# Cross attention with a gelu MLP on one core: the x loads moved to step 0, the x^T transposes behind them, two Strassen products swapped, and the read-out rows stored in one transfer

## The chip, the cores and the metric

The kernel runs on one core of a Trainium2 chip. The metric is the time of one execution on the device in microseconds (us). Every duration below is from one profiled execution of the kernel before, whose own time is 220.42 us.

## The reference

For each of 8 batches and 8 heads, x (512 rows of 64) attends to a state of 32 rows, and the state attends back to x. Both read-outs are joined (512 + 32 = 544 rows a batch, 512 columns) and go through a two-layer MLP with an exact gelu.

```
scores  = x @ state^T / 8 ;  a  = softmax(scores)  ; xread = a  @ state     # 512 rows a batch
scores2 = state @ x^T / 8 ;  a2 = softmax(scores2) ; sread = a2 @ x         # 32 rows a batch
X = concat([xread, sread]) as (8*544, 512)
out = gelu(X @ w_in) @ w_out          # w_in 512x2048, w_out 2048x512
```

## The kernel before, in words

The read-out is never formed for the 512 rows: P = state @ w_in is made per batch (`p_mm`, L415), and hidden = A @ P needs only A^T, the transposed softmax weights (`mm1`, L478, two matmuls for each of 16 blocks m; ScalarE applies the gelu, L485, into `g`). The second layer multiplies `g` by w_out. For batches 0 and 1 it is a plain product (`mm2`, L504). From batch 2 on it is one level of a Strassen scheme: seven products 3, 4, 5, 2, 1, 7, 6 of half size (`X`, matmuls L602), whose left sides are sums of parts of `g` (`g_sum`, VectorE, L596) and whose results are combined on their way out. Call them M1 to M7. Each has a fixed PSUM bank: M3 and M5 use bank 0, M4 and M2 bank 1, M1 and M7 bank 2, M6 bank 3. M7 accumulates onto what M1 left, so `q`, which reads M1 from the bank (L646), must have read it before M7 starts.

The order is written out by hand. The loop at L842 runs over slots b = 2 to 7. A slot has 8 steps p; a step runs two blocks of layer one of batch b (`M(k, k+1)`), and then one Strassen product of batch b-1 (steps 0 to 4) or of batch b (M3 at step 6, M6 at step 7). In its gaps a slot also prepares batch b+1 (scores at step 1, softmax norm at steps 2 and 3, A^T at step 5, P at steps 5 and 7) and loads x for batch b+3. Slot 1 is written the same way ahead of the loop (L817 to L840). In the profile, slot 2 starts at 58.7 us, slot 3 at 80.7, slot 4 at 103.2, slot 5 at 126.8 and slot 6 at 149.1.

What runs on the queues around the change:

- GpSimd (POOL): `load_x(b)` issues the x load of a batch (L117, 512 KB, with a cast to bf16), after a one-element copy to `hold` (L839, L880) that makes the queue wait for a gelu result. `rearr` copies x into the layout `x4` (L218, two copies), `rearr_ones` into `xo` (L228, two copies), and the Strassen terms `u` (L641) and `v` (L648) are subtractions.
- SyncE (SP) only issues transfers, in order: the DMA transposes xT <- x4 (L271, for the scores of that batch) and AT <- a (L367), and the stores of results. A transfer waits in the queue until its data is ready, and everything behind it waits too.
- VectorE (DVE) runs, among others, norm (cs, ics, a: L344 to L347), g_sum, q, the read-out pieces inv, srm and XSR (L391, L392, L405), the two final sums of a batch `oh` (L652, L656) and half of the P copies (L427).

Within slot b, step 0 begins with `rearr` and `xtr_dma` of batch b+2; step 2 ends with `rearr_ones` of batch b+2 and then `hold` (on gelu block 4 of the slot) and `load_x(b+3)`. After the loop come the last products and the 256 read-out rows: `mm2_sr(s)` for four batches at a time, which ends in `evac` (a copy out of PSUM and one store for each batch's 32 rows). `X7_split` stores the last half in pieces.

Of the kernel before, what the change touches and what calls it, by code (L numbers as in the profile page):

```python
# [9 lines left out]
FP32 = mybir.dt.float32  # L10
BF16 = mybir.dt.bfloat16
AF = mybir.ActivationFunctionType
ALU = mybir.AluOpType
# [4 lines left out]
def kernel(  # L18
# [8 lines left out]
    nc = tc.nc  # L27
# [87 lines left out]
    def load_x(b):  # L115
        xb = xin.tile([128, H, SJ * D], BF16, name="xb", tag="xb")
        nc.gpsimd.dma_start(out=xb, in_=xr[b])  # L117
        xbs[b] = xb
# [80 lines left out]
    def begin(b):  # L199
        A = Att()  # L200
        atts[b] = A
        A.x4 = x4s[b % 2]
        A.xo = xos[b % 2]
        if b > 0:
            A.xT = att.tile([128, SJ, HC, 128], BF16, name="xT", tag="xT")
# [8 lines left out]
    def rearr(b):  # L214
        A = atts[b]
        src = xbs[b].rearrange("p (t c) (j d) -> p t c j d", t=2, d=D)
        for t in range(2):
            nc.gpsimd.tensor_copy(  # L218
                out=A.x4[:, :, :, 64 * t:64 * t + 64].rearrange("p j c d -> p c j d"),
                in_=src[:, t],  # L220
            )
# [47 lines left out]
    def xtr_dma(b):  # L269
        A = atts[b]  # L270
        nc.sync.dma_start_transpose(  # L271
            out=A.xT.rearrange("p j c n -> p (j c) n"),
            in_=A.x4.rearrange("p j c n -> p (j c n)"),
        )
# [214 lines left out]
    def evac(ps, rows):  # L489
        osb = opool.tile([128, d_model], FP32, name="osb", tag="osb")  # L490
        nc.vector.tensor_copy(out=osb, in_=ps)
        for r, src, n0, n1 in rows:
            nc.sync.dma_start(out=r, in_=osb[src, n0:n1])
# [34 lines left out]
    def mm2_sr(s):  # L528
        ps = ps_f.tile([128, d_model], FP32, name="ops", tag="f")
        for m in range(MC):  # L530
            nc.tensor.matmul(  # L531
                ps,
                lhsT=g_sr[:, m, s * 128:(s + 1) * 128],
                rhs=w_out_bf[:, m, :],
                start=(m == 0),
                stop=(m == MC - 1),
            )
        rows = []
        for i in range(4):
            r0 = (4 * s + i) * SB + S  # L540
            rows.append((out[r0:r0 + NS, :], slice(32 * i, 32 * i + 32), 0, d_model))
        evac(ps, rows)


    def mm2_m(b, m):
# [65 lines left out]
    def c_tile(name):  # L611
        return cpool.tile([128, 2, NH], FP32, name=name, tag=name)

    def x_out(b, h):
        rows = out[b * SB:b * SB + S, :].rearrange("(p j) n -> p j n", j=SJ)
        nc.sync.dma_start(out=rows[:, 2 * h:2 * h + 2, :], in_=xs[b, "o", h])

    def X(b, name):
        bank = {"3": 0, "4": 1, "5": 0, "2": 1, "1": 2, "6": 3, "7": 2}[name]
        first = name in "3416"  # L620
        if first:
            xs[b, bank] = otile([128, 2, NH], "xp", bank)
        ps = xs[b, bank]
        lhs = {"3": (0, 0), "4": (1, 1)}.get(name)
        lhs = xs[b, "g" + name] if lhs is None else g_q(b, *lhs)
        rhs = {"5": w_q[1][1], "2": w_q[0][0]}.get(name)
        rhs = w_sum[name] if rhs is None else rhs
        x_mm(ps, lhs, rhs, first)
        if name == "3":
            xs[b, "s3"] = c_tile("s3")  # L630
            nc.scalar.copy(out=xs[b, "s3"], in_=ps)
            for h in range(2):
                xs[b, "o", h] = hpool.tile([128, 2, d_model], FP32, name="oh", tag=f"oh{h}")
        elif name == "4":
            xs[b, "s34"] = c_tile("s34")
            nc.vector.tensor_tensor(out=xs[b, "s34"], in0=ps, in1=xs[b, "s3"], op=ALU.add)  # L636
        elif name == "5":
            o = xs[b, "o", 0][:, :, NH:]
            nc.scalar.copy(out=o, in_=ps)  # L639
            xs[b, "u"] = c_tile("u")  # L640
            nc.gpsimd.tensor_tensor(out=xs[b, "u"], in0=xs[b, "s34"], in1=o, op=ALU.subtract)  # L641
        elif name == "2":
            nc.scalar.copy(out=xs[b, "o", 1][:, :, :NH], in_=ps)
        elif name == "1":
            xs[b, "q"] = c_tile("q")
            nc.vector.tensor_tensor(out=xs[b, "q"], in0=ps, in1=xs[b, "s34"], op=ALU.add)  # L646
            xs[b, "v"] = c_tile("v")
            nc.gpsimd.tensor_tensor(  # L648
                out=xs[b, "v"], in0=xs[b, "q"], in1=xs[b, "o", 1][:, :, :NH], op=ALU.subtract
            )  # L650
        elif name == "7":
            nc.vector.tensor_tensor(  # L652
                out=xs[b, "o", 1][:, :, NH:], in0=xs[b, 3], in1=xs[b, "v"], op=ALU.add
            )
            x_out(b, 1)
            nc.vector.tensor_tensor(  # L656
                out=xs[b, "o", 0][:, :, :NH], in0=ps, in1=xs[b, "u"], op=ALU.add
            )
            x_out(b, 0)
# [7 lines left out]
                out=xs[b, "q"][:, j, :], in0=ps[:, 0, :], in1=xs[b, "s34"][:, j, :], op=ALU.add  # L667
            )

    def c22(b):  # L670
        xs[b, "v"] = c_tile("v")
        o = xs[b, "o", 1]
        nc.gpsimd.tensor_tensor(
            out=xs[b, "v"], in0=xs[b, "q"], in1=o[:, :, :NH], op=ALU.subtract
        )
        nc.vector.tensor_tensor(out=o[:, :, NH:], in0=xs[b, 3], in1=xs[b, "v"], op=ALU.add)
        x_out(b, 1)

    def X7_split(b):
        rows = out[b * SB:b * SB + S, :].rearrange("(p j) n -> p j n", j=SJ)  # L680
        o = xs[b, "o", 0]
        nc.sync.dma_start(out=rows[:, 0:2, NH:], in_=o[:, :, NH:])
        for j in range(2):
            ps = xs[b, "x", j]
            x_mm(ps, xs[b, "g7"], w_sum["7"], False, (j,))
            nc.vector.tensor_tensor(
                out=o[:, j, :NH], in0=ps[:, 0, :], in1=xs[b, "u"][:, j, :], op=ALU.add
            )
            eng = nc.scalar if j else nc.sync
            eng.dma_start(out=rows[:, j, :NH], in_=o[:, j, :NH])  # L690
# [127 lines left out]
    for p in range(2, 8):  # L818
        if p == 4:
            scores(2, 0)  # L820
            scores(2, 1)
            norm(2, 0)
            norm(2, 1)
        if p == 7:
            atr_dma(2)
        if p == 3:
            begin(3)
            rearr(3)
            xtr_dma(3)
            rearr_ones(3)  # L830
        M(16 + 2 * p, 17 + 2 * p)
        U(u)
        u += 1
        if p in (5, 7):
            pmat(2, 2 + p // 7)
        if p >= 3:
            w_sums(p - 3)
        if p == 4:
            nc.gpsimd.tensor_copy(out=hold, in_=gs[1][:, 8, 0:1])  # L839
            load_x(4)  # L840

    for b in range(2, B):  # L842
        nb = b + 1
        for p in range(8):
            k = 16 * b + 2 * p
            if p == 0 and nb + 1 < B:
                begin(nb + 1)
                rearr(nb + 1)
                xtr_dma(nb + 1)
            if p == 1 and nb < B:  # L850
                scores(nb, 0)
                scores(nb, 1)
            if p in (2, 3) and nb < B:
                norm(nb, p - 2)
            if p == 5 and nb < B:
                atr_dma(nb)
            M(k, k + 1)
            if nb == B and p >= 4:
                for m in range(4 * p - 16, 4 * p - 12):
                    mm1_sr(m)  # L860
            if b == 2:
                for _ in range(2 if p < 4 else 1):
                    if u < 32:
                        U(u)
                        u += 1
            elif p < 5:
                if p == 0:
                    g_sum(b - 1, "5")
                X(b - 1, "45217"[p])
                if p < 3:  # L870
                    g_sum(b - 1, "217"[p])
            if p == 1:
                sread(b)
                sread_out(b)
            if p == 2 and nb + 1 < B:
                rearr_ones(nb + 1)
            if p == 2 and b + 3 < B:


                nc.gpsimd.tensor_copy(out=hold, in_=gs[b][:, 4, 0:1])  # L880
                load_x(b + 3)
            if p == 3:
                srt(b)
            if p == 5:
                g_sum(b, "6")
                if nb < B:
                    p_run(nb, (0, 1), ((0, 1), (3, 2)))
            if p == 6:
                X(b, "3")
            if p == 7:  # L890
                if nb < B:
                    p_run(nb, (2, 3), ((1, 2), None))
                X(b, "6")
# [4 lines left out]
    g_sum(b, "2")  # L898
    mm2_sr(0)
    X(b, "5")  # L900
    g_sum(b, "7")
    X1_split(b)
    X(b, "2")
    c22(b)
    mm2_sr(1)
    X7_split(b)

# [29 lines left out]
```

## Time and profile before

| what | value |
|---|---|
| median of 11 runs | 220.2 us (217.53 to 221.2) |
| profiled execution | 220.42 us, of which the span from first to last instruction is 218.7 us |
| TensorE (PE) busy | 202.8 us, 93% of the span |
| ScalarE (ACT), VectorE (DVE), GpSimd (POOL) busy | 131.4, 127.8, 65.6 us |
| share of the chain that ended last | PE 75%, DVE 9%, DMA 8% |
| PE waiting for AT <- a, in all | 4.3 us in 2 waits |
| PE waiting for q of VectorE, in all | 2.3 us in 3 waits |

Times in timeline lines are us from the start of the span, then the duration, the engine, the line, the operation, `out<-in`, shapes, how many; in brackets the idle time of the engine ahead of it and what ended it. SPq is SyncE's queue of transfers. A line of the waits reads: who waited, for whom, us in all, how often, the longest.

### The profile page before, as it was taken

The numbers are of one execution on the slowest core, as the hardware profiler recorded it, in microseconds if no ns is written. First come the engines' busy times: TensorE is split into PE (matmuls) and PEld (weight loads), VectorE is DVE, ScalarE is ACT, GpSimd is POOL, SyncE is SP. The second block draws the span as 40 slices with busy tenths as digits, with TensorE's granted clock in tenths as the row PEclk, the third lists the DMA queues.
The fourth block names the chain that finished last, engine by engine and source line by source line (L and its number), as shares of the span: only waits on it lengthen the run. The fifth ranks groups of instructions, "written<-read, shape, count | busy, mean of one in ns | idle before, by whom it ended". The sixth has DMA issues, their size and how long they took to land.

```text
span 218.7 us, 4614 instructions
## 1 busy us (share of the span) xinstructions
PE 202.8 (93%) x1939; PEld 128.3 (59%) x1939; DVE 127.8 (58%) x206; ACT 131.4 (60%) x237; POOL 65.6 (30%) x71
## 2 busy tenths in 40 slices
PE   7799999998499999989998989899999999999990
PEld 6545444443144467746774657657775777786850
DVE  2935665739407846975597538755875572325530
ACT  3845855779286669556964768387848555860110
POOL 8954304901306120933084305500220022000320
PEclk9999999999889999999999999999999999999997
DMA  6999999973751990089107930070007000400124
GB/s 202 178 179 204 206 193 150 232 153 37 110 96 5 236 194 3 0 139 273 23 3 100 262 72 3 1 240 3 1 3 240 3 0 34 161 0 0 51 102 140
DMA packets 37957, 23.14 MB, mean 106 GB/s; under 512 B 21808, under 2 KB 35376, under 8 KB 37936
## 3 DMA queue, kind: packets, MB, share of 16 engines
q0 software_dynamic: 13936, 8.10, 27.6%
q1 hardware_dynamic: 23312, 14.29, 25.0%
q10 hardware_dynamic: 688, 0.46, 0.7%
q8 instruction: 15, 0.25, 0.5%
q14 instruction: 6, 0.05, 0.1%
HBM read 17.30 MB, written 8.91 MB: 120 GB/s over the span
## 4 chain that ended last, share of the span: by engine, by line
PE 75%; DVE 9%; DMA 8%; ACT 3%; issue 1%; POOL 1%; SPq 0%; ACTq 0%
PE xp L602 28%; PE hp L478 20%; PE op L504 8%; DMA AT<-a 7%; PE p_ps L415 4%; PE hps L519 3%; PE op L549 3%; PE ops L531 3%; DVE gsum L596 3%; DVE a L347 2%; DMA x0f<-in_x_dram 2%; DVE cs L344 2%; PE sr L378 1%; PE pt L324 1%; DVE q L646 1%
## 5 line engine op out<-in xcount | busy, mean ns | idle before, releaser
L485 ACT ACTIVATE g<-hp 128x512 bf16<-128x512 f32 x124 | 67.6, 603 | 41.0 <-PE hp L478 36.2
L478 PE MATMUL hp<-AT,P 128*128 128x512 bf16 x248 | 64.8, 384 | 4.4 <-DMA AT<-a 4.3
L602 PEld LDWEIGHTS <-gsum 128*128 128x128 bf16 x480 | 46.5, 98 | 14.7 <-issue 5.4
L596 DVE TENSOR_TENSOR gsum<-g 128x2048 bf16<-128x2048 bf16 x30 | 39.6, 1335 | 7.9 <-ACT g L485 6.8
L478 PEld LDWEIGHTS <-P 128*128 128x128 bf16 x248 | 22.2, 98 | 26.0 <-DMA AT<-a 5.0
L602 PE MATMUL xp<-ws,gsum 128*128 128x256 bf16 x288 | 34.4, 273 | 2.3 <-DVE q L646 2.3
L641 POOL TENSOR_TENSOR u<-s,oh 128x512 f32<-128x512 f32 x6 | 8.0, 1331 | 80.8 <-ACT oh L639 80.8
L427 DVE CAST P<-p_ps 128x512 bf16<-128x512 f32 x31 | 20.0, 684 | 18.5 <-PE p_ps L415 18.5
L504 PE MATMUL op<-w_out_bf,g 128*128 128x512 bf16 x96 | 24.4, 388 | 0.0
L602 PE MATMUL xp<-w_out_bf,gsum 128*128 128x256 bf16 x192 | 22.9, 273 | 0.0
L602 PE MATMUL xp<-ws,g 128*128 128x256 bf16 x192 | 22.9, 273 | 0.0
L602 PEld LDWEIGHTS <-g 128*128 128x128 bf16 x192 | 18.8, 98 | 4.3
L218 POOL COPY x<-xb 128x1024 bf16<-128x1024 bf16 x12 | 12.1, 1041 | 30.6 <-DMA xb<-in_x_dram 30.6
L426 ACT CAST P<-p_ps 128x512 bf16<-128x512 f32 x31 | 17.0, 604 | 7.0 <-PE p_ps L415 7.0
L228 POOL COPY xo<-xb 128x1024 bf16<-128x1024 bf16 x12 | 16.6, 1409 | 5.9 <-PE sr L378 5.9
L504 PEld LDWEIGHTS <-g 128*128 128x128 bf16 x96 | 9.4, 100 | 12.4 <-issue 2.6
L636 DVE TENSOR_TENSOR s<-xp,s 128x512 f32<-128x512 f32 x6 | 4.2, 692 | 15.5 <-PE xp L602 15.5
L347 DVE TENSOR_TENSOR a<-e,ics 128x512 bf16<-128x512 bf16 x14 | 12.1, 865 | 0.6 <-DVE ics L346 0.2
L344 DVE TENSOR_REDUCE cs<-e 128x16 f32<-128x512 bf16 x14 | 9.5, 676 | 3.4 <-ACT e L331 3.4
L415 PE MATMUL p_ps<-w_in_bf,sbd 64*32 64x512 bf16 x248 | 10.7, 382 | 0.6 <-ACT g L485 0.5
L648 POOL TENSOR_TENSOR v<-q,oh 128x512 f32<-128x512 f32 x5 | 6.3, 1267 | 11.0 <-DVE XSR L405 11.0
L331 ACT ACT_TABLE_LOAD x7 | 9.0, 1283 | 0.6 <-PE pt L324 0.5
(93 smaller groups left out, 194.7 us busy)
## 6 DMA issues: line engine op xcount, KB each, us to landing
out_dram<-oh SPq DMA_DIRECT2D x11, 512.0 KB, 3.5
xb<-in_x_dram POOLq DMA_DIRECT2D x7, 512.0 KB, 7.4
w_out_bf<-in_moe_w_out_dram POOLq DMA_DIRECT2D x4, 512.0 KB, 12.6
out_dram<-osb SPq DMA_DIRECT2D x7, 256.0 KB, 3.9
w_in_bf<-in_moe_w_in_dram POOLq DMA_DIRECT2D x6, 256.0 KB, 11.9
x0f<-in_x_dram SPq DMA_DIRECT2D x3, 256.0 KB, 3.8
w_in_bf<-in_moe_w_in_dram POOLq DMA_DIRECT2D x4, 128.0 KB, 4.1
out_dram<-osb SPq DMA_DIRECT2D x8, 64.0 KB, 1.7
```

What stands on the lines that cost most here:

```text
L218: nc.gpsimd.tensor_copy(out=A.x4[:, :, :, 64 * t:64 * t + 64].rearrange("p j c d -> p c j d"), in_=src[:, t],)
L228: eng.tensor_copy(out=A.xo[:, :, :, 2 + 64 * t:66 + 64 * t].rearrange("p j c d -> p c j d"), in_=src[:, t],)
L344: nc.vector.reduce_sum(out=cs, in_=e4, axis=AX.X)
L347: nc.vector.tensor_tensor(out=A.a[:, :, hs].rearrange("p g (c n) -> p g c n", n=NS), in0=e4, in1=ics[:, :, :].to_broadcast((128, G, 2, NS) ...
L415: nc.tensor.matmul(ps[t][32 * c:32 * c + 32, :], lhsT=sbd[64 * t:64 * t + 64, b, c, 32 * t:32 * t + 32], rhs=w_in_bf[64 * t:64 * t + 64, c ...
L426: nc.scalar.copy(out=dst[:, 0, :], in_=ps[0])
L427: nc.vector.tensor_copy(out=dst[:, 1, :], in_=ps[1])
L478: nc.tensor.matmul(hp, lhsT=Ps[b][:, t, m * 128:(m + 1) * 128], rhs=atts[b].AT[:, :, t, :], start=(t == 0), stop=(t == 1),)
L485: nc.scalar.activation(out=gs[b][:, m, :], in_=hp, func=AF.Gelu)
L504: nc.tensor.matmul(ps, lhsT=gs[b][:, m, j * 128:(j + 1) * 128], rhs=w_out_bf[:, m, :], start=(m == 0), stop=(m == MC - 1),)
L596: nc.vector.tensor_tensor(out=t, in0=g_q(b, h0, k0), in1=g_q(b, h1, k1), op=op)
L602: nc.tensor.matmul(ps[:, j - js[0], :], lhsT=lhs[:, m, 128 * j:128 * j + 128], rhs=rhs[:, m, :], start=(first and j == js[0] and m == 0), ...
```

## The change

1. In a slot, `hold` and `load_x(b+3)` move from step 2 to step 0, after the step's product, and wait for gelu block 0 of the slot in place of block 4. In slot 1 the load of x for batch 4 moves from step 4 to step 2 (gelu block 4 in place of 8).
2. `begin` and `rearr` of batch b+2 move behind that load, within step 0; `xtr_dma` moves from step 0 to step 3.
3. M1 is computed at step 2 and M2 at step 3 (they were the other way round). `v`, the final sum that needs it and the store of that half move into M2's step (`c22`), where they stood at M1 and M7.
4. `mm2_sr` stores its four batches' rows in one transfer of 128 rows, in place of four of 32 rows.
5. The store of the right half of the last rows is issued after M5 in the tail, where it stood in `X7_split`, behind the stores of the second `mm2_sr`.

```diff
@@ mm2_sr
-        rows = []
-        for i in range(4):
-            r0 = (4 * s + i) * SB + S
-            rows.append((out[r0:r0 + NS, :], slice(32 * i, 32 * i + 32), 0, d_model))
-        evac(ps, rows)
+        osb = opool.tile([128, d_model], FP32, name="osb", tag="osb")
+        nc.vector.tensor_copy(out=osb, in_=ps)
+        nc.sync.dma_start(
+            out=out.rearrange("(b s) n -> b s n", s=SB)[4 * s:4 * s + 4, S:SB, :], in_=osb
+        )
@@ X
         elif name == "2":
             nc.scalar.copy(out=xs[b, "o", 1][:, :, :NH], in_=ps)
+            c22(b)
         elif name == "1":
             xs[b, "q"] = c_tile("q")
             nc.vector.tensor_tensor(out=xs[b, "q"], in0=ps, in1=xs[b, "s34"], op=ALU.add)
-            xs[b, "v"] = c_tile("v")
-            nc.gpsimd.tensor_tensor(
-                out=xs[b, "v"], in0=xs[b, "q"], in1=xs[b, "o", 1][:, :, :NH], op=ALU.subtract
-            )
         elif name == "7":
-            nc.vector.tensor_tensor(
-                out=xs[b, "o", 1][:, :, NH:], in0=xs[b, 3], in1=xs[b, "v"], op=ALU.add
-            )
-            x_out(b, 1)
             nc.vector.tensor_tensor(
                 out=xs[b, "o", 0][:, :, :NH], in0=ps, in1=xs[b, "u"], op=ALU.add
             )
@@ X7_split
-        nc.sync.dma_start(out=rows[:, 0:2, NH:], in_=o[:, :, NH:])
@@ slot 1
-        if p == 4:
-            nc.gpsimd.tensor_copy(out=hold, in_=gs[1][:, 8, 0:1])
+        if p == 2:
+            nc.gpsimd.tensor_copy(out=hold, in_=gs[1][:, 4, 0:1])
             load_x(4)
@@ slots 2 to 7
-            if p == 0 and nb + 1 < B:
-                begin(nb + 1)
-                rearr(nb + 1)
-                xtr_dma(nb + 1)
...
+            if p == 3 and nb + 1 < B:
+                xtr_dma(nb + 1)
...
-                X(b - 1, "45217"[p])
+                X(b - 1, "45127"[p])
                 if p < 3:
-                    g_sum(b - 1, "217"[p])
+                    g_sum(b - 1, "127"[p])
...
+            if p == 0 and b + 3 < B:
+                nc.gpsimd.tensor_copy(out=hold, in_=gs[b][:, 0, 0:1])
+                load_x(b + 3)
+            if p == 0 and nb + 1 < B:
+                begin(nb + 1)
+                rearr(nb + 1)
             if p == 2 and nb + 1 < B:
                 rearr_ones(nb + 1)
-            if p == 2 and b + 3 < B:
-                nc.gpsimd.tensor_copy(out=hold, in_=gs[b][:, 4, 0:1])
-                load_x(b + 3)
@@ tail
     X(b, "5")
+    nc.sync.dma_start(
+        out=out[b * SB:b * SB + S, :].rearrange("(p j) n -> p j n", j=SJ)[:, 0:2, NH:],
+        in_=xs[b, "o", 0][:, :, NH:],
+    )
...
     X(b, "2")
-    c22(b)
```

`c22` itself is unchanged: `v` on GpSimd, the final sum on VectorE, `x_out(b, 1)` on SyncE. It stood in the tail alone and now ends every M2.

More of the change, by code (lines that the diff above doesn't have):

```diff
@@ L616, in x_out, with c22 @@
         nc.sync.dma_start(out=rows[:, 2 * h:2 * h + 2, :], in_=xs[b, "o", h])
+    def c22(b):
+        xs[b, "v"] = c_tile("v")
+        o = xs[b, "o", 1]
+        nc.gpsimd.tensor_tensor(
+            out=xs[b, "v"], in0=xs[b, "q"], in1=o[:, :, :NH], op=ALU.subtract
+        )
+        nc.vector.tensor_tensor(out=o[:, :, NH:], in0=xs[b, 3], in1=xs[b, "v"], op=ALU.add)
+        x_out(b, 1)
     def X(b, name):
@@ L668, in X1_split @@
             )
[L670 to L677, printed above, removed]
     def X7_split(b):
@@ L900 @@
     X(b, "5")
+    nc.sync.dma_start(
+        out=out[b * SB:b * SB + S, :].rearrange("(p j) n -> p j n", j=SJ)[:, 0:2, NH:],
+        in_=xs[b, "o", 0][:, :, NH:],
+    )
     g_sum(b, "7")
```

## The prediction

> **What bounds the kernel now.** I read the page's busy shares first (PE 93%, nothing else above 60%), then who PE waited for, the granted clock around the longest wait, and the timelines of the places where these waits lie.
>
> PE's own waits, from 50 us on:
>
> ```profile
> PE hp L478 <- DMA AT<-a: 4.3, 2, 3.3
> PE xp L602 <- DVE q L646: 2.3, 3, 0.8
> ```
>
> So the loop has two kinds of hole: A^T comes late (once 3.27, once 1.03 us), and M7 waits for q in slots 3 to 5 (about 0.76 each). Everywhere else PE is the bound, and only its instruction count would help, which the change leaves as it is.
>
> The longest hole is at the start of slot 2 (timeline):
>
> ```profile
> 50.47 0.19 POOL L839 COPY hold<-g 128x1 bf16<-128x1 bf16 x1 [6.93 <-ACT g L485]
> 50.97 0.87 POOL L117 DMA_DIRECT2D xb<-in_x_dram  x1 [0.31 <-POOL hold L839]
> 51.42 1.23 SPq L367 DMA_TRANSPOSE AT<-a  x1
> 58.72 1.89 PE L478 MATMUL hp<-AT,P 128*128 128x512 bf16 x4 [3.27 <-DMA AT<-a]
> ```
>
> The x load and the transpose were issued 0.45 us apart; both landed just before 58.7 (7.4 and 7.3 us). The same transpose issued at 75.19 landed in 4.0 us. Then the clock (columns: window, length, busy time with instruction counts of PE, PEld, DVE, ACT, POOL, the granted PE clock, DMA share, GB/s):
>
> ```profile
> 55.40:58.70 3.30, 0.05 (x8) 0.00 (x0) 1.82 (x2) 0.59 (x1) 0.27 (x1) 0.96 1.01 143
> 58.70:60.60 1.90, 1.88 (x5) 0.73 (x6) 0.00 (x0) 0.60 (x1) 1.75 (x2) 0.50 0.00 0
> 60.60:63.00 2.40, 2.40 (x15) 0.99 (x13) 0.00 (x0) 1.88 (x2) 0.00 (x0) 0.74 0.62 116
> ```
>
> After the hole PE ran at 0.50 and 0.74 of its clock. After the 1.03 us hole at 126.78 it did not: four hp took 1.04 us, as everywhere.
>
> The end of step 3 and step 4 in slot 3:
>
> ```profile
> 89.12 3.48 POOL L228 COPY xo<-xb 128x1024 bf16<-128x1024 bf16 x2
> 89.64 2.05 DVE L596 TENSOR_TENSOR gsum<-g 128x2048 bf16<-128x2048 bf16 x1
> 93.22 0.68 DVE L646 TENSOR_TENSOR q<-xp,s 128x512 f32<-128x512 f32 x1
> 93.95 1.91 PE L602 MATMUL xp<-ws,gsum 128*128 128x256 bf16 x16 [0.76 <-DVE q L646]
> 95.95 0.68 DVE L656 TENSOR_TENSOR oh<-xp,u 128x512 f32<-128x512 f32 x1
> 96.10 0.89 SPq L616 DMA_DIRECT2D out_dram<-oh  x2
> 97.08 2.13 SPq L367 DMA_TRANSPOSE AT<-a  x1
> ```
>
> q stands behind norm and g_sum in DVE's queue, and the g_sum took 2.05 us beside GpSimd's copies, against 1.22 elsewhere. And the tail:
>
> ```profile
> 212.23 1.74 SPq L493 DMA_DIRECT2D out_dram<-osb  x4
> 212.38 0.43 DVE L686 TENSOR_TENSOR oh<-xp,u 128x256 f32<-128x256 f32 x1 [0.18 <-PE xp L602]
> 213.71 0.37 ACTq L690 DMA_DIRECT2D out_dram<-oh  x1
> 214.01 0.43 SPq L682 DMA_DIRECT2D out_dram<-oh  x1
> 214.55 0.44 SPq L690 DMA_DIRECT2D out_dram<-oh  x1
> ```
>
> The store of the first piece has its data at 212.81 and is issued at 214.55, behind five others; it lands 3.2 us later, at 217.7, the last of all.
>
> **Part A, the load in slot 1.** Gelu block 4 of slot 1 (ACT 42.82, two blocks in 1.09) is ready at 43.4, so hold, the load's issue (0.3 + 0.87) and the two x4 copies of batch 3 (2.03) end near 46.9. The load takes 5.8 to 7.4 us and lands by 51.4. What is moved past it: the copies of batch 3 come 5.3 us later (39.54 before) and so does the issue of xT(3) (42.32 before, 3.72 long), now 46.9 to 50.6. That ends ahead of AT(2)'s issue at 51.42, which stays where `a` ends. DVE has no norm until 48.05, so the copies block nothing there; the last ends at 48.9, ahead of `a` at 49.05. xT(3) itself is read at 62.85, so its 5 us are covered. AT(2) alone: 51.42 + 4.0 = 55.4, and PE is ready at 58.72 - 3.27 = 55.45. Removed: 3.27 of waiting, and the slow clock, 1.90 x 0.50 + 2.40 x 0.26 = 1.57. Together 4.8. From both sides: 0 if AT still takes 7.3 us, 4.8 at best, since PE is next.
>
> **Part B, AT(5) at 119.57.** It took 7.2 us, with the x load landing at 120.9, 1 MB of stores ahead of it on the same queue, and xT(7) issued at 123.03 behind it; in slot 6 (143.10), with the stores alone, 4.4. The load moves to the start of the slot, but in slot 5 there is no load and no hold: x4(7) stands first in GpSimd's queue, runs as soon as v of slot 4 is done, and SyncE issues xT(7) straight behind AT(5). So one of two disturbers stays. Between 0 and 1.03 I take 0.5. AT(4) in slot 3 (6.0 us) had 0.1 us to spare and gets more: worth nothing.
>
> **Part C, M1 ahead of M2.** M1 now ends at 89.5 in slot 3, norm's `a` at 89.7, q follows at once (0.68, to 90.4), then g_sum for M7 (1.2, or 2.05 beside the xo copies: 92.5 at the latest). M7 can start at 93.0: the wait of 0.76 goes in slots 3 to 5, 2.3 in all. What is late next: v must wait for M2 (PE to 92.1), ScalarE's copy (0.59) and the xo copies (92.6), so it runs from about 92.8 to 94.1, or 94.5 if the `a` of norm blocks it. Behind v on DVE stand the first oh (0.69), XSR (0.21) and the second oh (0.68): 96.1 at the latest. P's second chunk at step 5 writes the two banks that these oh read; PE gets there at 95.9 in the new count. I charge 0.3 in each of three slots: 2.3 - 0.9 = 1.4. At best 2.3; from below, if v slips 1 us more, 1.4 - 3.0 = -1.6. The x4 copies now run at step 0 beside two g_sums (2.35 together, up to 0.83 more each by the 2.05 row). Those are needed one and two steps (2.6 us each) later; that covers them. Without the cover, q slips by up to 1.7, its wait (0.76) returns and adds to the -1.6 end. XSR is read only in the last slot, and the planner gives the hp after it another PSUM buffer, so nobody waits for it.
>
> **Part D, the tail.** SyncE issues one store where it issued four (1.74 us), and the right half went out long before. The first piece, ready at 212.81, is issued at about 212.9 and lands by 216.1 with the 3.2 of its row. The ScalarE piece lands at 213.71 + 2.2 = 215.9. The merged store (256 KB, 4 batches x 32 rows) is in no row. The nearest is the 256 KB osb store of 128 rows, 3.3 to 3.9 us at 39.7 to 42.2; at most it would be four 64 KB stores in a row, 4 x 1.7 = 6.8. I take 3.9, the same bytes and row length: 212.23 + 3.9 = 216.1. The last landing moves from 217.7 to 216.1: 1.6 (best 1.8; worst 212.23 + 6.8 = 219.0, a loss of 1.3).
>
> The Trainium skill speaks against this piece. "DMA: Bandwidth & Descriptors", section "Why a DMA increments its semaphore by 16 and not by 1", says that a transfer runs on the largest number of engines, up to 16, that divides the slowest dimension of both sides. Here that is 4 batches against 128 partitions, so 4 engines. With that page's 27 GiB/s an engine and 2 us fixed, an estimate is 4.3 us, 216.5, and D would be 1.2; the sum would be 212.5. No row here shows a store with an outer dimension of 4.
>
> **Sum.** 4.8 + 0.5 + 1.4 + 1.6 = 8.3 us off the profiled execution's 220.42 (span 218.7 and 1.7 around it), so 212.1. That execution stands 0.2 above the median of 220.2, within the spread.
>
> **Rivals.**
>
> 1. *The hole at slot 2 stays, with xT(3) in the load's place.* xT(3) now runs beside the load (the transposes took 4.2 alone, 5.3 behind stores); if it is still in flight at 53, AT(2) takes 7 us again. For: AT(5) took 7.2 with a transpose behind it. Against: 4.5 us lie between the two issues. A is then 0: 220.42 - 3.5 = 216.9.
> 2. *The transposes are not one by one after all.* Nothing waits for a landing; only the place in the queue changes. If AT(5) still meets xT(7) for its full 7.2 us, and PE reaches it earlier by what it no longer loses, B is -0.5: 213.1.
> 3. *Slower: VectorE stands still for v.* The first oh waits for v with XSR, the second oh and the P copies behind it, in slots 3 to 7; the second store and AT follow the second oh on SyncE. It decides where each of the five slots loses over 8.3 / 5 = 1.7 us beyond the count above, that is v ending after 96.2 in slot 3. At 2.5 a slot it is 12.5 - 8.3 = 4.2 us slower, 224.6. For: DVE waited 1.3 us for v in each slot already. Against: POOL is 30% busy, and v's last input comes at 92.8.
>
> **How the numbers follow.** Forecast with rival 2 as its near neighbour: 0.72. Rival 1: 0.17. Rival 3, or anything of its size: 0.09, and 0.02 for nothing in between. The range: best ends 4.8 + 1.0 + 2.3 + 1.8 = 9.9 give 210.5, and 0.5 below for spread; the upper end takes rival 1, 217.0, and leaves out rival 3. About 0.5% (1.1 us) is what can be told from no change: faster 0.88, same 0.03, slower 0.09.
>
> **What would show it.** A: the x load issued near 44, no PE wait for AT at slot 2 over 0.5 us, the clock 1.00 through 55 to 60. B: AT(5) landing in under 6 us. C: no PE wait for q; instead short ones of p_ps for oh. D: two SyncE stores fewer between 212 and 215, and the merged store's landing time. It is wrong if AT(2) still lands after 7 us, if PE waits for oh by more than 1 us a slot, or if the merged store ends last by far.

## The result, and the profile after

The median went from 219.98 us (47 runs, 217.53 to 223.39) to 217.03 us (12 runs, 215.48 to 218.45): a ratio of 0.988, 95% interval 0.986 to 0.991. So the change is faster, by 2.95 us and not by the 8.3 of the forecast. Here and below a ratio leaves out the runs that lie over 1.5% above the fastest of their kernel, so it can differ a little from that of the medians (here it says 1.2%, some 2.5 us). The profiled execution took 217.4 us, with a span of 215.6 (218.7 before). TensorE is still the bound, at 94% of the span.

I read the waits of PE first, as before. A line reads: who waited, for whom, us in all, how often, the longest.

```profile
PE hps L519 <- DVE XSR L405: 2.0, 1, 2.0
PE warm_ps L146 <- DVE warm L92: 1.0, 1, 1.0
...
```

Both holes of before have left the list: no wait for A^T, none for q. A wait that was not there before leads it, for XSR. The holes were worth the following. The starts of the slots on PE are from the timelines of both kernels, before and after:

| | slot 2 | slot 3 | slot 4 | slot 5 | slot 6 | slot 7 | PE's last end | span's end |
|---|---|---|---|---|---|---|---|---|
| before | 58.72 | 80.74 | 103.16 | 126.78 | 149.12 | 170.60 | 213.23 | 218.65 |
| after | 55.18 | 75.67 | 97.33 | 119.33 | 140.78 | 162.22 | 208.51 | 215.63 |
| won so far | 3.5 | 5.1 | 5.8 | 7.5 | 8.3 | 8.4 | 4.7 | 3.0 |

At the start of slot 7 the change had won 8.4 us. From there to PE's end it lost 3.7, and between PE's end and the last landing another 1.7. These two losses are what has to be explained.

First what was won. The timeline of after, at the load in slot 1 and at AT(5) in slot 4:

```profile
44.05 0.87 POOL L117 DMA_DIRECT2D xb<-in_x_dram  x1
46.97 3.33 SPq L271 DMA_TRANSPOSE xT<-x  x1
51.21 2.04 SPq L367 DMA_TRANSPOSE AT<-a  x1
55.18 1.04 PE L478 MATMUL hp<-AT,P 128*128 128x512 bf16 x4
...
113.21 1.91 SPq L367 DMA_TRANSPOSE AT<-a  x1
115.22 3.63 SPq L271 DMA_TRANSPOSE xT<-x  x1
119.33 1.04 PE L478 MATMUL hp<-AT,P 128*128 128x512 bf16 x4
```

The load is issued at 44.05 and lands 6.3 us later, xT(3) takes 6.8 beside it, and AT(2), issued at nearly the same time as before, lands in 3.4 us where it took 7.3. PE goes on without a hole (no bracket behind its matmuls). AT(5) still has xT(7) issued 2 us behind it and takes 6.07. PE's last matmul before it ends at 119.20 and AT(5) lands at 119.28, so some 0.1 us of that hole is left, too little for the list.

Slot 3, from M2 to the first P copy of step 5:

```profile
85.55 0.68 DVE L656 TENSOR_TENSOR q<-xp,s 128x512 f32<-128x512 f32 x1
86.15 1.46 DVE L596 TENSOR_TENSOR gsum<-g 128x2048 bf16<-128x2048 bf16 x1
87.91 1.27 POOL L621 TENSOR_TENSOR v<-q,oh 128x512 f32<-128x512 f32 x1 [1.37 <-ACT oh L652]
87.96 1.91 PE L602 MATMUL xp<-ws,gsum 128*128 128x256 bf16 x16
89.64 0.68 DVE L624 TENSOR_TENSOR oh<-xp,v 128x512 f32<-128x512 f32 x1
90.37 0.68 DVE L658 TENSOR_TENSOR oh<-xp,u 128x512 f32<-128x512 f32 x1
90.66 0.85 PE L415 MATMUL p_ps<-w_in_bf,sbd 64*32 64x512 bf16 x16
```

q now runs 2.4 us before M7 (87.96), which starts without a wait. The 16 matmuls into the two banks that the `oh` read took 0.85 us in place of 0.63.

Now what was lost. The same places in slot 7:

```profile
173.13 0.22 PE L402 MATMUL srT<-ident,srm 128*128 128x128 bf16 x1
173.37 0.58 ACT L652 COPY oh<-xp 128x512 f32<-128x512 f32 x1 [1.14 <-issue]
174.04 1.26 POOL L621 TENSOR_TENSOR v<-q,oh 128x512 f32<-128x512 f32 x1 [4.42 <-ACT oh L652]
175.33 0.69 DVE L624 TENSOR_TENSOR oh<-xp,v 128x512 f32<-128x512 f32 x1 [2.79 <-POOL v L621]
175.94 0.21 DVE L405 COPY XSR<-srT 128x128 bf16<-128x128 bf16 x1
176.21 2.63 PE L519 MATMUL hps<-XSR,w_in_bf 128*128 128x256 bf16 x16 [2.00 <-DVE XSR L405]
178.64 2.91 PE L602 MATMUL xp<-ws,gsum 128*128 128x256 bf16 x16
```

The input of XSR is there at 173.4, but VectorE's next instruction is the final sum that now ends M2, and it waits 2.79 us for v, which waits for ScalarE's copy of M2. XSR stands behind it. In slots 2 to 6 XSR has no hurry. In slot 7 it has: there is no next batch to prepare, and step 4 runs the first layer of the read-out rows (`mm1_sr`, L519), which reads XSR. PE waits 2.00 us, with a slow clock behind. Windows of after (window, length, busy time with instruction counts of PE, PEld, DVE, ACT, POOL, the granted PE clock, DMA share, GB/s):

```profile
55.00:58.00 3.00, 3.00 (x28) 1.40 (x21) 1.98 (x3) 2.67 (x4) 1.40 (x2) 1.00 0.00 0
172.00:176.00 4.00, 2.21 (x17) 1.36 (x15) 1.21 (x3) 1.81 (x4) 1.26 (x1) 1.00 0.00 0
176.00:179.00 3.00, 2.79 (x18) 2.17 (x19) 0.16 (x2) 1.27 (x4) 0.00 (x0) 0.71 0.43 175
179.00:181.60 2.60, 2.60 (x18) 1.86 (x16) 0.02 (x1) 0.27 (x1) 0.00 (x0) 0.68 0.00 0
```

The first row is slot 2, at full clock now. After the wait in slot 7 the clock is 0.71 and 0.68: 3.0 x 0.29 + 2.6 x 0.32 = 1.7 us. With the 2.0 of waiting that is the 3.7 of the table. It shows in the matmuls too: the 16 of L602 at 178.64 took 2.91 us, where 16 of them take 1.91 elsewhere.

The tail of after, timeline and windows:

```profile
207.53 0.56 SPq L540 DMA_DIRECT2D out_dram<-osb  x1
208.18 0.42 SPq L682 DMA_DIRECT2D out_dram<-oh  x1
209.01 0.36 ACTq L682 DMA_DIRECT2D out_dram<-oh  x1
```

```profile
208.50:210.00 1.50, 0.02 (x1) 0.00 (x0) 0.43 (x1) 0.00 (x0) 0.00 (x0) 1.00 0.36 38
210.00:211.50 1.50, 0.00 (x0) 0.00 (x0) 0.00 (x0) 0.00 (x0) 0.00 (x0) 0.96 0.74 198
211.50:213.00 1.50, 0.00 (x0) 0.00 (x0) 0.00 (x0) 0.00 (x0) 0.00 (x0) 0.50 0.27 95
```

SyncE issues its piece at 208.18, 0.1 us after its data, as forecast. But the two pieces, 128 KB each, land 5.3 and 4.8 us after their issue (2.2 to 3.2 before), at 213.5 and 213.8. From 211.5 on the busy share of the 16 DMA engines is only 0.27, which is as much as 4.3 of them, moving 95 GB/s. The packet records of the trace agree: the merged store's packets, 2 KB each, run mostly four and never more than five at a time, from 208.7 to 212.8 us, and the last packets of the two pieces run four at a time until 213.5. In the kernel before, the same 128 packets, from four stores, run up to 16 at a time and take 1.9 us in all. The records do not name the engines.

### The profile page after: what moved, and what is told of

It reads as the page before. It is cut to its first block, busy times and chain, and to the rows that moved or that the text cites. A ratio compares the mean times of both kernels' runs of the same rounds, so it can differ in the third digit from the quotient of the medians.

```text
span 215.6 us, 4608 instructions
## 1 busy us (share of the span) xinstructions
PE 203.7 (94%) x1939; PEld 129.7 (60%) x1939; DVE 128.9 (60%) x206; ACT 131.4 (61%) x237; POOL 65.0 (30%) x71
## 4 chain that ended last, share of the span: by engine, by line
PE 84%; POOL 5%; DMA 3%; ACT 3%; issue 1%; DVE 1%; POOLq 0%; ACTq 0%
PE xp L602 33%; PE hp L478 24%; PE op L504 9%; PE p_ps L415 4%; PE hps L519 4%; PE op L549 3%; PE ops L531 3%; DMA AT<-a 3%; POOL w_in_bf L105 2%; PE pt L324 1%; PE sr L378 1%; POOL sbd L95 1%; ACT g L485 1%; PE hp L748 1%; ACT L485 1%
## 5 line engine op out<-in xcount | busy, mean ns | idle before, releaser
L478 PE MATMUL hp<-AT,P 128*128 128x512 bf16 x248 | 63.9, 380 | 0.3
L602 PEld LDWEIGHTS <-gsum 128*128 128x128 bf16 x480 | 47.1, 99 | 12.5 <-issue 2.1
L602 PE MATMUL xp<-ws,gsum 128*128 128x256 bf16 x288 | 35.4, 277 | 0.0
L504 PE MATMUL op<-w_out_bf,g 128*128 128x512 bf16 x96 | 23.7, 379 | 0.0
L602 PE MATMUL xp<-w_out_bf,gsum 128*128 128x256 bf16 x192 | 22.9, 273 | 0.0
L602 PE MATMUL xp<-ws,g 128*128 128x256 bf16 x192 | 22.9, 273 | 0.0
L602 PEld LDWEIGHTS <-g 128*128 128x128 bf16 x192 | 18.8, 98 | 4.3
L218 POOL COPY x<-xb 128x1024 bf16<-128x1024 bf16 x12 | 12.6, 1082 | 11.3 <-DMA xb<-in_x_dram 11.3
L228 POOL COPY xo<-xb 128x1024 bf16<-128x1024 bf16 x12 | 14.5, 1240 | 1.3 <-PE sr L378 1.3
L347 DVE TENSOR_TENSOR a<-e,ics 128x512 bf16<-128x512 bf16 x14 | 13.8, 986 | 0.5
L621 POOL TENSOR_TENSOR v<-q,oh 128x512 f32<-128x512 f32 x6 | 7.7, 1281 | 13.4 <-ACT oh L652 13.4
L415 PE MATMUL p_ps<-w_in_bf,sbd 64*32 64x512 bf16 x248 | 11.2, 382 | 0.6 <-ACT g L485 0.5
L866 POOL COPY hold<-g 128x1 bf16<-128x1 bf16 x3 | 1.0, 331 | 31.1 <-ACT g L485 31.1
```

The lines of the kernel that those rows point to most:

```text
L218: nc.gpsimd.tensor_copy(out=A.x4[:, :, :, 64 * t:64 * t + 64].rearrange("p j c d -> p c j d"), in_=src[:, t],)
L228: eng.tensor_copy(out=A.xo[:, :, :, 2 + 64 * t:66 + 64 * t].rearrange("p j c d -> p c j d"), in_=src[:, t],)
L347: nc.vector.tensor_tensor(out=A.a[:, :, hs].rearrange("p g (c n) -> p g c n", n=NS), in0=e4, in1=ics[:, :, :].to_broadcast((128, G, 2, NS) ...
L415: nc.tensor.matmul(ps[t][32 * c:32 * c + 32, :], lhsT=sbd[64 * t:64 * t + 64, b, c, 32 * t:32 * t + 32], rhs=w_in_bf[64 * t:64 * t + 64, c ...
L478: nc.tensor.matmul(hp, lhsT=Ps[b][:, t, m * 128:(m + 1) * 128], rhs=atts[b].AT[:, :, t, :], start=(t == 0), stop=(t == 1),)
L504: nc.tensor.matmul(ps, lhsT=gs[b][:, m, j * 128:(j + 1) * 128], rhs=w_out_bf[:, m, :], start=(m == 0), stop=(m == MC - 1),)
```

## The experiments

Theory after this reading: the loop kept its gain; (1) XSR behind v in slot 7 costs about 3.7 us, and (2) the merged store costs about 1.7 and more, because it lies on about four engines and the pieces issued behind it wait there. The rivals: that the slow clock in slot 7 has another cause than the wait, that the late pieces come from the new place of the right half's store, and that the parts hinder each other in the loop.

**XSR ahead of the final sum.** The `srT` transpose and XSR move ahead of M2 in step 3, so that XSR precedes the final sum in VectorE's queue.

```diff
@@ slots, after M(k, k + 1)
+            if p == 3:
+                srt(b)
...
-            if p == 3:
-                srt(b)
```

> The changed kernel, with the transpose and the copy of the read-out sums (srT, XSR) moved at step 3 ahead of M2, so that XSR stands in VectorE's queue ahead of the sum that waits for v. Theory 1 (in slot 7 PE waits 2.0 us for XSR, which stands behind the wait for v, and then runs at 0.7 of its clock for some 5.6 us): the wait goes and the clock stays at 1.00, 2.0 + 1.6 = 3.6 us less than the changed kernel, about 213.4. Rival (PE would wait there anyway, for v or for the gelu of the read-out rows, XSR being only the last of several): less than 1 us less, and a new wait in its place.

Measured: 214.48 us, ratio to before 0.976 (0.969 to 0.982); span 212.7; some 1 us above what was expected. The timeline in slot 7:

```profile
173.43 0.22 DVE L405 COPY XSR<-srT 128x128 bf16<-128x128 bf16 x1
175.02 1.91 PE L519 MATMUL hps<-XSR,w_in_bf 128*128 128x256 bf16 x16
175.06 1.27 POOL L621 TENSOR_TENSOR v<-q,oh 128x512 f32<-128x512 f32 x1 [4.47 <-ACT oh L652]
176.36 0.69 DVE L624 TENSOR_TENSOR oh<-xp,v 128x512 f32<-128x512 f32 x1 [2.72 <-POOL v L621]
```

VectorE waits for v as long as before (2.72), but XSR is through and PE does not wait; the 16 matmuls take 1.91 in place of 2.63. From the start of slot 7 to PE's end it is 42.45 us here (163.19 to 205.64), against 46.29 in the changed kernel and 42.63 in the kernel before. The loss in slot 7 is gone with XSR's place in the queue: the 2.0 of waiting, and in this execution the slow clock too. (Not every such wait brings the slow clock, as the next run shows.) The tail stayed as in the changed kernel: pieces landing after 5.3 and 4.8 us. The gain over the changed kernel is 1.3% by the two ratios (2.8 us). It is not the whole 3.8 between the profiles. This profiled execution came to slot 7 some 1.0 us later: 0.7 by slot 2 (in the first stage it waited 0.8 us for a load of w_out that the changed one's did not wait for) and 0.3 by a wait for AT(5).

**The four stores back.** The changed kernel with the store of the read-out rows as it was, XSR left late.

```diff
@@ mm2_sr
-        osb = opool.tile([128, d_model], FP32, name="osb", tag="osb")
-        nc.vector.tensor_copy(out=osb, in_=ps)
-        nc.sync.dma_start(
-            out=out.rearrange("(b s) n -> b s n", s=SB)[4 * s:4 * s + 4, S:SB, :], in_=osb
-        )
+        rows = []
+        for i in range(4):
+            r0 = (4 * s + i) * SB + S
+            rows.append((out[r0:r0 + NS, :], slice(32 * i, 32 * i + 32), 0, d_model))
+        evac(ps, rows)
```

> The changed kernel, with the read-out rows stored again by four transfers of 32 rows; everything else as changed. Theory 2 (the merged store runs on a few DMA engines only and the last pieces queue behind it: 7.1 us from PE's end to the end of the span, 5.4 before): the first piece is issued near PE's end and lands in about 3 us, the tail is 3.7 to 4.5 us long, 2.6 to 3.4 us less than the changed kernel, about 214. Rival (the tail is long because everything is issued on one queue, whatever the shape): the tail stays above 6.5 us, under 0.6 us less.

Measured: 213.56 us, ratio 0.973 (0.965 to 0.982); span 210.8. Landings of the last two pieces (the line gives shortest, median and longest), first in the changed kernel, then in this one:

```profile
DMA to landing us min/median/max: 4.8/5.1/5.3
```

```profile
DMA to landing us min/median/max: 2.1/2.1/2.1
```

The time from PE's last end to the span's end is 3.9 us, against 7.1 in the changed kernel and 5.4 before. The right half's early store is in this kernel too, so that was not the cause. The wait for XSR is still 2.0 us, but in the profiled execution the clock did not fall after it, and slot 7 to PE's end took 44.63 us, which is 1.66 less than in the changed kernel with its slow clock. This kernel's four times (212.4, 212.6, 214.5, 214.8) stand in two pairs some 2 us apart, not far from the 1.7 us that the slow clock cost. The two longer ones also have the lower mean clock (0.988 and 0.990, against 0.997 and 0.998). What decides whether the clock falls is in the last section.

**Both mends together.** The two diffs above in one kernel.

> Both edits on the changed kernel: XSR ahead of M2 and four stores of 32 rows. If both theories hold and add up: 3.6 + 3.0 = 6.6 us less than the changed kernel, about 210.4. If the tail hides part of the first (a shorter loop only reaches a tail that is as long), it is 212 or more.

Measured: 211.0 us, ratio 0.959 (0.954 to 0.965), span 209.3, clock 1.00 over the whole span. Its tail:

```profile
204.45 1.75 SPq L493 DMA_DIRECT2D out_dram<-osb  x4
205.94 0.36 ACTq L682 DMA_DIRECT2D out_dram<-oh  x1
206.31 0.36 SPq L682 DMA_DIRECT2D out_dram<-oh  x1
```

SyncE's piece goes out at 206.3, some 1.3 us after its data (VectorE's sum, 204.60 + 0.42), behind the four stores; it lands in 2.1 us. This is the best version: 9.5 us faster than the 220.48 of the kernel before on that chip.

**The last stores on two queues.** The best version, with the last two of the four stores issued on ScalarE, so that SyncE's piece waits less for its turn. The diff is against the changed kernel; `srt` stands ahead of M2 as in the best version.

```diff
@@ mm2_sr
-        nc.sync.dma_start(
-            out=out.rearrange("(b s) n -> b s n", s=SB)[4 * s:4 * s + 4, S:SB, :], in_=osb
-        )
+        for i in range(4):
+            r0 = (4 * s + i) * SB + S
+            eng = nc.scalar if s == 1 and i >= 2 else nc.sync
+            eng.dma_start(out=out[r0:r0 + NS, :], in_=osb[32 * i:32 * i + 32, :])
```

> Both repairs (XSR ahead of M2, four stores), and of the last four stores two are issued by ScalarE. If the tail is now bound by SyncE's issues (four stores and a piece, 2.2 us from the first issue to the last), the last piece is issued 0.8 us earlier and it takes 0.4 to 0.8 us less than with all four on SyncE, about 210.3. If landing is what counts, no change: 211.0.

Measured: 211.31 us, ratio 0.959 (0.955 to 0.964), span 209.5: no gain. SyncE's piece goes out at 205.24, about 1 us earlier, but ScalarE's piece, issued at 205.81, now lands 2.8 us later, at 208.6. In the best version the last piece lands at 208.4. The place in SyncE's queue no longer decides the end.

**The swap alone.** The kernel before with M1 ahead of M2 and `c22` at M2, nothing else.

```diff
@@ slots 2 to 7 (c22 at M2 as in the change)
-                X(b - 1, "45217"[p])
+                X(b - 1, "45127"[p])
                 if p < 3:
-                    g_sum(b - 1, "217"[p])
+                    g_sum(b - 1, "127"[p])
...
```

> The kernel before, with only M1 ahead of M2 (and v, its sum and its store behind M2). Theory 1: it takes 2.2 us of waits for q out of slots 3 to 5 and puts 3.5 us into slot 7 (wait for XSR, slow clock): 1.3 us slower than before, about 221.3. Rival (the loss in slot 7 comes from the earlier loads or the new store, not from the swap): 2.2 us faster, about 217.8.

Measured: 221.1 us, ratio 1.000 (0.995 to 1.005). The waits, and the windows behind the one for XSR, which ends at 182.47:

```profile
PE hp L478 <- DMA AT<-a: 4.5, 3, 3.0
PE hps L519 <- DVE XSR L405: 2.0, 1, 2.0
```

```profile
182.40:184.40 2.00, 1.93 (x18) 1.75 (x19) 0.01 (x1) 1.15 (x3) 0.00 (x0) 1.00 0.62 258
184.40:187.00 2.60, 2.60 (x22) 1.95 (x21) 0.83 (x2) 0.78 (x2) 0.00 (x0) 1.00 0.01 3
```

The 2.3 us of waiting for q are gone and 2.0 for XSR stand in their place: the swap brings the wait for XSR by itself, without the moved loads. Alone it is worth nothing. And the clock stayed at 1.00 after the same 2.0 us of waiting.

**The load of slot 1 alone.** The kernel before with only the load of x(4) at step 2.

```diff
-        if p == 4:
-            nc.gpsimd.tensor_copy(out=hold, in_=gs[1][:, 8, 0:1])
+        if p == 2:
+            nc.gpsimd.tensor_copy(out=hold, in_=gs[1][:, 4, 0:1])
```

> The kernel before, with only the x load of slot 1 two steps earlier. Theory A (the load and AT(2) share the DMA engines at the start of slot 2): AT(2) lands in about 4 us, the wait of 3.3 us goes and with it the slow clock after it (1.6 us); 4.8 us less than before, about 215.6. Rival (what is removed there comes back at slot 4 or 5, where AT(5) is late anyway): 3 us or less.

Measured: 215.13 us against 220.65 of the kernel before on the same chip, ratio 0.975 (0.972 to 0.979). AT(2) landed in 3.3 us. Two lines of the diff are worth 5.5 us, about twice what the whole change brought.

```profile
PE xp L602 <- DVE q L646: 2.3, 3, 0.8
PE hp L478 <- DMA AT<-a: 1.3, 1, 1.3
```

What stays is what parts B and C were for.

**The slots' loads alone.** The kernel before with `hold`, load, `begin`, `rearr` and `xtr_dma` of slots 2 to 7 moved as in the change, slot 1 and the order of the products as before.

```diff
@@ slots 2 to 7 (the old places taken out, as in the change)
+            if p == 3 and nb + 1 < B:
+                xtr_dma(nb + 1)
...
+            if p == 0 and b + 3 < B:
+                nc.gpsimd.tensor_copy(out=hold, in_=gs[b][:, 0, 0:1])
+                load_x(b + 3)
+            if p == 0 and nb + 1 < B:
+                begin(nb + 1)
+                rearr(nb + 1)
```

> The kernel before, with only the loads and the x^T transposes of slots 2 to 7 moved as in the change. Theory B (the load beside AT(5) is what PE waits for at slot 5): the wait of 1.0 us at slot 5 goes, AT(5) lands in about 6 us. But the x4 copies at step 0 then push norm and q back by up to 0.8 us in slots 3 and 4, where M7 waits for q in this order, 1.6 us. Together 0.5 us slower than before, within noise. Rival (the copies are covered, as the prediction has it): 1.0 us less.

Measured: 221.69 us, ratio 1.006 (1.002 to 1.010): slightly slower.

```profile
PE xp L602 <- DVE q L646: 4.3, 3, 1.8
PE hp L478 <- DMA AT<-a: 3.3, 1, 3.3
```

AT(5) landed in 6.3 us and its wait is gone, but the x4 copies now run beside two g_sums at step 0, q comes later, and with M1 still behind M2 PE waits for it 2.0 us more in all. In the changed kernel M1 comes a step earlier, and nobody sees that delay: B pays only with C beside it. (C does take the waits for q out by itself, as the swap alone shows, and loses about as much in slot 7.)

**The merged store alone.** The kernel before with the one store for four batches of the change (its `mm2_sr`), and nothing else.

> The kernel before, with only the four stores of read-out rows merged into one, the right half still behind it. Theory 2 (few DMA engines carry it, and every later store on the queue waits for its share on them): from its issue near 212.2 to the end of the span some 8.1 us, as in the changed kernel, so 1.7 us slower than before, about 222. Rival (SyncE's four issues were the cost): the pieces are issued 1.3 us earlier and it is 1 us or more faster.

Measured: 223.2 us against 220.65, ratio 1.011 (1.008 to 1.015): slower by 2.5 us, more than the loss seen in the changed kernel, where the right half's store had gone out early. The tail:

```profile
212.82 0.55 SPq L540 DMA_DIRECT2D out_dram<-osb  x1
213.42 0.47 SPq L682 DMA_DIRECT2D out_dram<-oh  x1
213.99 0.42 SPq L690 DMA_DIRECT2D out_dram<-oh  x1
214.30 0.36 ACTq L690 DMA_DIRECT2D out_dram<-oh  x1
```

All three pieces go out within 1.5 us of the merged store, as the diff suggests, and land 5.5, 5.7 and 5.4 us after their issue, the last two at 219.7; in the kernel before, the last landed at 217.7. The loss belongs to the merged store and to nothing else of the change.

The parts alone sum to -2.46% (slot 1), +0.58% (slots' loads), -0.02% (swap) and +1.14% (store): -0.8%, where the whole is -1.16%. The right half's early store was not run alone.

## Why the prediction was wrong in its size, step by step

- **Part A, right.** Forecast 4.8: the wait of 3.27 and the slow clock of 1.57. The table shows 3.5 at slot 2 and 5.1 at slot 3, and the load of slot 1 alone shows it too. AT(2) took 3.4 where I took 4.0. Rival 1 is out, though its condition was met: xT(3) was in flight until 53.8, and AT(2) landed 0.8 us behind it, at 54.6.
- **Part B, right, taken too low.** Between 0 and 1.03 I took 0.5; the hole of 1.03 went but for about 0.1. AT(5) took 6.07 and not under 6, and PE was there 0.1 before it landed (0.2 to 0.3 in the three versions with XSR ahead of the final sum). The load was one disturber: AT(5) took 7.1 to 7.4 in the four kernels with a load in flight and 6.1 to 6.3 in the six without. That xT(7) is the other is not shown (last section). What the part rests on is the cover that Part C names for the slowed g_sums. The two at step 0 of slots 3 and 4 took 3.65 and 3.74 together, where they took 2.35; the slots' loads alone show what that costs without the cover: M7 waits for q 1.75 and 1.79 us in slots 3 and 4, 1.0 more in each, where Part C had put the slip at up to 1.7 in each.
- **Part C, right in slots 3 to 5, wrong in slot 7.** Slots 3 to 5 won 0.8, 1.6 and 0.9 by the table. Less the 0.9 of Part B that is 2.3 to 2.4 for the swap, the whole 2.3 and not the 1.4 that were left after my charge. The charge was there in slots 3 and 4 (the P matmuls took 0.85 and 0.89 for 0.63) and not in slot 5; where the rest of it was made good I did not trace. The sentence that failed is "XSR is read only in the last slot, and the planner gives the hp after it another PSUM buffer, so nobody waits for it". I had listed XSR among what stands behind v, but did not walk the last slot, where its reader is PE itself, one step later. The order written by hand says it in two lines (`if nb == B and p >= 4`, `mm1_sr(m)`). Cost: 2.0 of waiting and, in the profiled execution, 1.7 of clock. It is rival 3's mechanism, VectorE standing still for v, at the one place where I had not priced it; in the other slots it cost 0.3 at most.
- **Part D, wrong in sign.** Forecast a gain of 1.6, measured a loss of 1.7. The failed step is the row: I took the 3.9 us of a 128-row store for the merged one because bytes and row length were the same, and let the pieces behind it keep their 2.2 and 3.2. I asked when the merged store lands, and not what it does to the transfers behind it. Working it from the windows: between 211.5 and 213.0 about four engines moved 95 GB/s. If four of 16 engines carry the 256 KB and a quarter of the two pieces, they have 256 + 64 = 320 KB, which at that rate is 3.4 us, against 1.4 if 16 engines shared all of the 512 KB at four times the rate. This division is an estimate; the packets show it longer, since the merged store's own are spread over 4.1 us (208.7 to 212.8).
- **The skill's rule that spoke against Part D held.** "DMA: Bandwidth & Descriptors" in the Trainium skill, section "Why a DMA increments its semaphore by 16 and not by 1", has a transfer run on the largest number of engines, up to 16, that divides the slowest dimension of both sides, here 4. The DMA share of 0.27 agrees, and so do the packets, four at a time; 95 GB/s on about 4.3 engines is 22 GB/s each, under the page's 27 GiB/s. But my estimate by that page, 4.3 us, was still too short: it priced the store by itself. With the two pieces beside it the store's last packet ended 5.3 us after its issue, and the last piece landed 1.0 us after that.
- **A gain of that size in the tail is there, by another path.** With the four stores back and the right half out early, PE's end to the span's end is 3.9 us against 5.4 before. But SyncE's piece does not go out at once, as forecast: it waits some 1.3 us behind the four stores and then lands in 2.1 us, not 3.2. That 1.5 is near the forecast 1.6 is luck, and that it comes from the right half's early store is argued, since that edit was not run alone.

So against the 8.3 forecast, the loop gave 8.4 (forecast 6.7), slot 7 took back 3.7 (forecast 0) and the tail 1.7 (forecast a gain of 1.6). With both undone the kernel is 9.5 us faster.

## What to carry to other kernels

When an instruction that waits moves up in an engine's queue, list what now stands behind it, and look up the readers of each in the first and the last pass of the loop too, not in a middle one: the boundary passes run other work in the gaps. Fewer transfers are not shorter transfers: look at the outermost dimension of the merged one, and price the small transfers that are issued right behind it, for they land after it. And an edit that is harmful alone (here the slots' loads) can pay beside another (the swap) that takes off the path what the first one slows.

## What was not expected of the hardware

- The granted clock after a wait of PE of 2.0 us fell to 0.71 and 0.68 in the changed kernel, and stayed at 1.00 after the same wait in the kernel with the swap alone and in that with the four stores. After 3.27 us it fell (0.50, 0.74), after 1.03 us it did not. The clock records of the ten traces show what decides. The granted clock changes only at the edges of a grid of 3.41 us: stretches of one clock last, for instance, 3.41, 30.72, 54.61 or 204.8 us, whole multiples of it. The grid lies elsewhere in each execution. In the changed kernel the whole wait fell into one interval, and the next was granted half the clock; with the four stores an edge cut the wait into 1.1 and 0.9 us. Windows set on the grid, the first two of the changed kernel, the others of that with the four stores:

```profile
173.85:177.26 3.41, 1.41 (x12) 0.95 (x11) 0.82 (x2) 1.48 (x4) 1.26 (x1) 1.00 0.10 43
177.26:180.67 3.41, 3.41 (x19) 2.36 (x17) 0.00 (x0) 1.15 (x3) 0.00 (x0) 0.50 0.27 111
172.00:175.41 3.41, 2.30 (x18) 1.43 (x16) 0.63 (x1) 1.90 (x4) 1.26 (x1) 1.00 0.00 0
175.41:178.82 3.41, 2.52 (x23) 2.27 (x24) 0.82 (x2) 1.54 (x4) 0.00 (x0) 1.00 0.37 154
```

In all ten traces, once the clock was first full, every interval with 2.00 us or more of idle PE was followed by one at 0.50, and none with 1.94 us or less was. So the 2.0 us of waiting for XSR, the same in all three traces that have it, costs a further 1.7 us (half of 3.41) only where the grid happens to lie so.

- A DMA transpose in flight ahead of another on the same queue did not slow it (AT(2): 3.4 us, with xT(3) landing 0.8 us earlier). AT(5) took 6.07 with 1 MB of stores ahead and xT(7) issued 2 us behind, but that either is the reason is not shown: AT(6) took 4.1 with the same stores ahead, AT(4) took 5.6 with those stores and no transpose behind it, and in the kernel with the load of slot 1 alone AT(2) took 3.3 with a transpose issued 1.4 us behind it. With no x load in flight, in the ten traces, a 16 KB packet of the queue that the profile calls "instruction" (q8) started 1.6 us or more into each AT that took 5.5 us or longer, and into none of those that took 4.5 or less. No run tests this.
- A store of 128 KB on ScalarE's queue landed late (4.8 us, 2.2 before) behind a merged store issued on SyncE's queue: here another queue was no way round the busy engines.
